# A fused attention, soft-MoE and top-1 MoE kernel: a new hand-written order, queries in four even quarters, an early exponential and shorter reader-less products

## The chip, the cores and the metric

The kernel runs on one core of a Trainium2 chip. The metric is the device time of one execution in microseconds (us). Engines are named as in the profile: PE (matrix products; PEld its weight loads), DVE (vector), ACT (scalar, exponentials), POOL (general), SP (here only the queue that issues most transfers).

## The reference, cut to what matters

```python
# q, k, v: (8 batches, 8 heads, 576 tokens, 64); x below: (4608 tokens, 512)
q_s = softmax(q, axis=-1)                    # over the 64 features
k_s = softmax(k, axis=2)                     # over the 576 tokens
kv  = einsum('bhsd,bhse->bhde', k_s, v)
x   = einsum('bhsd,bhde->bhse', q_s, kv)     # -> (4608, 512)

logits = x @ phi                             # (4608, 32): 8 experts x 4 slots
d = softmax(logits, axis=0)                  # over the tokens
slot_input = (d.T @ x).reshape(8, 4, 512)
for e in range(8):
    slot_out[e] = relu(slot_input[e] @ w1[e]) @ w2[e]
x = softmax(logits, axis=1) @ slot_out.reshape(32, 512)

g = x @ w_gate;  e_idx = argmax(g)           # a second MoE, top-1
gate = max softmax(g); eom = sigmoid(x @ w_output_gate)
out[token] = gate * eom[e_idx] * (relu(x @ m1[e_idx]) @ m2[e_idx])
```

Shapes: w1 is (8, 512, 1024), w2 is (8, 1024, 512), m1 and m2 are of the same shapes. All of it is float32.

## The kernel before

**Units.** The attention is done in 8 units of two batches by four heads; units 2p and 2p+1 (the two halves of the heads) make pair p, that is 1152 tokens. One load each of k, q and v for a unit is 1152 KB; after them come the 32 halves of expert weights (`lw.0` to `lw.31`, 1024 KB each, two of w1 and two of w2 for each expert), and late in the program the weights of the one expert that the second MoE picks (`lm`, `ln`). All these loads go through the queue of SP in the order in which the program writes them, and each load is written into a named buffer, its home. A home is used again and again: `W_HOMES` says into which buffer `lw.i` goes, and SP holds the load back until the last instruction that reads the old contents is done. Behind it every later load waits too. In the order before, `lw.9` goes to the buffer k0, which holds the v of unit 6 until then, last read by the product `kv.6.3`.

**Order.** Nothing is scheduled automatically. `ORDER` (attention and slots), `TAIL` (experts and the routing) and `LAST` are strings of short names; `do` walks through them and emits the instructions, and each engine runs its own in that order. After a colon stand the buffer of PSUM, the home or the engine of a copy (A is ACT, D is DVE):

```python
        for op in order.split():
            n, _, x = op.partition(":")
            n, *i = n.split(".")
            ops[n](*map(int, i), *(x.split(",") if x else ()))
```

The names that matter here, for unit u: `kmax`, `kexp` (DVE maximum, ACT exponential of k), `ktr`, `kev` (PE transposes and their copies to SBUF), `kv.u.x` (four groups of ten small products), `kve` (copy), `kvb`, `km`; for q `qmax`, `qsub` (POOL), `qexp`, `qsum`, `qrec`, `qmul` (POOL), `qtr`, `qev`; `lg` (logits of the pair into PSUM, bank L0). For a pair: `lmax`, `lexp`, `lcp` (a copy of the logits), `ll` (36 small products that turn the logits token by token), `le` (their copy to `l_all`), `ltr` and `lev` (transposes of the exponentials and their copy to `dz`), `su` (slot sums U), `m1` to `m6`, `uev`, `st`, `ute`, `sa`, `sc` (running maximum and sums over pairs). The last pair's `sc.3` closes `ORDER`; then come the experts: `i`, `in`, `j` (w1 products), `o` (w2 products), `G` (the routing that picks the expert whose weights `lm` and `ln` then load).

**Reader-less products.** `h` (function `hot`) writes products of a zero tile (`zero`) into a bank that nobody reads; `h.1.22` is 22 of 512 columns in bf16 and one of 264.

**Logits before.** A pair's 1152 tokens stand in four groups of PSUM partitions with 256, 320, 320 and 256 columns (`SEGS`), in a strip `LW` = 384 columns wide, of which the unused places hold -1e30 (a memset of `lp`).

**Output loop.** 36 tiles of 128 tokens, in 12 groups of three; each tile is four products of 512 columns; `drain` scales it (ACT and DVE in turn) and a store of 768 KB follows for each group. The last group's stores go out tile by tile.

**Constants.** The constants are built ahead of the manual schedule (`msched`), and the framework places them: three that are made from `ident` stand behind the first maxima of k on DVE.

## Time and profile before

| what | value |
|---|---|
| median of 3 runs | 220.82 us (220.55 to 221.08) |
| the profiled execution's own time | 220.66 us |
| its span in the trace | 218.9 us |
| PE busy | 207.6 us (95%) |
| DVE busy | 164.5 us (75%) |
| ACT busy | 115.8 us (53%) |
| POOL busy | 95.2 us (43%) |
| DMA | 76.30 MB, of it 66.42 MB read from HBM |
| granted TensorE clock, mean | 0.997 |

The span is what the hardware profiler saw from the first instruction to the last; the time of the execution is 1.76 us longer, and the prediction adds that to the span. Shares are means over a program with three stages: attention (to about 117 us), experts and routing (to about 177 us) and the output loop. PE's share holds the reader-less products too.

### The profile page before, as it was taken

The numbers are of one execution on the slowest core, as the hardware profiler recorded it, in microseconds if no ns is written. First come the engines' busy times: TensorE is split into PE (matmuls) and PEld (weight loads), VectorE is DVE, ScalarE is ACT, GpSimd is POOL, SyncE is SP. The second block draws the span as 40 slices with busy tenths as digits, with TensorE's granted clock in tenths as the row PEclk, the third lists the DMA queues.
The fourth block names the chain that finished last, engine by engine and source line by source line (L and its number), as shares of the span: only waits on it lengthen the run. The fifth ranks groups of instructions, "written<-read, shape, count | busy, mean of one in ns | idle before, by whom it ended". The sixth has DMA issues, their size and how long they took to land.

```text
span 218.9 us, 6486 instructions
## 1 busy us (share of the span) xinstructions
PE 207.6 (95%) x2649; PEld 151.5 (69%) x2649; DVE 164.5 (75%) x345; ACT 115.8 (53%) x262; POOL 95.2 (43%) x109
## 2 busy tenths in 40 slices
...
GB/s 225 425 423 421 418 419 414 419 419 417 417 423 412 412 415 424 394 106 418 428 415 418 413 416 419 418 412 422 403 410 164 0 52 252 249 268 237 287 276 165
DMA packets 12208, 76.30 MB, mean 349 GB/s; under 512 B 1488, under 2 KB 1872, under 8 KB 5392
## 3 DMA queue, kind: packets, MB, share of 16 engines
...
q10 hardware_dynamic: 288, 0.39, 0.5%
...
HBM read 66.42 MB, written 9.44 MB: 347 GB/s over the span
## 4 chain that ended last, share of the span: by engine, by line
PE 68%; DMA 22%; DVE 4%; ACT 2%; issue 1%; ACTq 1%; SPq 1%
DMA vz<-in_v_dram 9%; PE kv L284 7%; DMA we<-in_w_dram 7%; DMA vz<-in_w_dram 6%; PE p L393 5%; PE kv L1512 5%; PE L L1512 4%; PE p L261 4%; PE U L458 4%; PE U L644 3%; PE L L413 3%; PE U L795 2%; PE U L1512 2%; PE p L743 2%; PE kv L795 2%; PE kv L743 2%
## 5 line engine op out<-in xcount | busy, mean ns | idle before, releaser
L359 POOL TENSOR_TENSOR qt<-qt,qm 128x1280 f32<-128x1280 f32 (+1 forms) x14 | 29.5, 2118 | 14.0 <-DVE rk L310 8.0
L385 POOL TENSOR_TENSOR qt<-qt,qi 128x1280 f32<-128x1280 f32 (+1 forms) x14 | 29.5, 2117 | 2.9 <-DVE qi L374 1.9
L251 ACT ACTIVATE kt<-kt,km 128x576 f32<-128x576 f32 x28 | 21.6, 779 | 0.0
L244 DVE TENSOR_REDUCE km<-kt 128x4 f32<-128x2304 f32 (+1 forms) x10 | 18.1, 1823 | 3.1 <-DMA kt<-in_k_dram 3.1
L367 DVE TENSOR_REDUCE qeps<-qt 128x20 f32<-128x1280 f32 (+1 forms) x14 | 18.7, 1337 | 0.2 <-ACT qt L363 0.2
L772 POOL MEMSET hte<- 128x256 f32 x8 | 2.5, 315 | 37.7 <-DVE den L561 18.4
L352 DVE TENSOR_REDUCE qm<-qt 128x20 f32<-128x1280 f32 (+1 forms) x14 | 18.5, 1329 | 0.1
L363 ACT ACTIVATE qt<-qt 128x1280 f32<-128x1280 f32 (+1 forms) x14 | 16.2, 1178 | 2.7 <-POOL qt L359 2.6
L284 PE MATMUL kv<-ek,vt 128*64 128x64 f32 x384 | 15.5, 225 | 0.1
L284 PEld LDWEIGHTS kv<-ek,vt 128*64 128x64 f32 x384 | 13.2, 138 | 2.8 <-issue 2.4
L235 ACT COPY eT<-p 128x512 f32<-128x512 f32 (+1 forms) x22 | 11.6, 556 | 6.2 <-PE p L393 6.1
L261 PE MATMUL p<-ident,kt 128*128 128x128 f32 x98 | 14.1, 278 | 0.7 <-ACT kt L251 0.6
L393 PE MATMUL p<-ident,qt 128*128 128x128 f32 x96 | 13.6, 276 | 0.3 <-POOL qt L385 0.3
L644 PE MATMUL U<-zero 128*128 128x512 bf16 x42 | 11.7, 444 | 1.1 <-DVE zero L168 1.1
L261 PEld LDWEIGHTS p<-ident,kt 128*128 128x128 f32 x98 | 10.8, 140 | 2.6 <-ACT kt L251 1.3
L1512 PE MATMUL kv<-mst,hr 128*128 128x512 f32 (+1 forms) x30 | 11.6, 387 | 0.0
L1512 PE MATMUL L<-mst,hr 128*128 128x512 f32 (+1 forms) x30 | 11.5, 383 | 0.0
L393 PEld LDWEIGHTS p<-ident,qt 128*128 128x128 f32 x96 | 10.7, 142 | 1.0 <-POOL qt L385 0.5
L413 PE MATMUL L<-eT,mq 128*32 128x256 f32 (+1 forms) x128 | 10.8, 411 | 0.0
L458 PE MATMUL U<-qt,dz 128*32 128x256 f32 x140 | 10.7, 383 | 0.0
L644 PEld LDWEIGHTS <-zero 128*128 128x128 bf16 x49 | 5.4, 112 | 7.4 <-issue 3.0
L235 ACT COPY ek<-p 128x512 f32<-128x512 f32 x17 | 9.7, 585 | 0.9 <-PE p L261 0.9
...
## 6 DMA issues: line engine op xcount, KB each, us to landing
...
```

Source lines behind the costliest of these rows:

```text
L235: nc.scalar.copy(out=o, in_=i)
L251: nc.scalar.activation(out=t, in_=t, func=AF.Exp, bias=st_["km", u][:, x:x + 1], accum_out=st_["ksum", u][:, x:x + 1])
L261: nc.tensor.transpose(t[:, n * P:(n + 1) * P], ks_[u][:, j * P:(j + 1) * P], ident)
L284: nc.tensor.matmul(o[D * hh:D * hh + D, x * D:x * D + D], vt[:, f:f + D], kk, start=(n == 0), stop=(n == 4))
L352: nc.vector.tensor_reduce(out=m[:, :n], in_=t.rearrange("p (x d) -> p x d", d=D), op=ALU.max, axis=AX.X)
L359: nc.gpsimd.tensor_tensor(out=t, in0=t, in1=m.unsqueeze(2).to_broadcast([P, n, D]), op=ALU.subtract)
L367: nc.vector.tensor_reduce(out=qeps[u % 2 * 2 + x][:, :n, 0], in_=t.rearrange("p (x d) -> p x d", d=D), op=ALU.add, axis=AX.X)
L385: nc.gpsimd.tensor_tensor(out=t, in0=t, in1=s.unsqueeze(2).to_broadcast([P, n, D]), op=ALU.mult)
L393: nc.tensor.transpose(t[:, n * P:(n + 1) * P], qs_[u][:, o:o + P], ident)
L458: nc.tensor.matmul(U[NS * g:NS * g + NS, hf * HH * D:(hf + 1) * HH * D], dz[:, blk * P + NS * g:blk * P + NS * g + NS], t[:, j * HH * D:(j ...
L644: nc.tensor.matmul(scratch.rearrange("p (a b) -> p a b", a=2), zero[:, :P], zero[:, :2 * P].unsqueeze(1).to_broadcast([P, 2, 2 * P]), star ...
L1512: nc.tensor.matmul(op, a[:, x], w[:, d0:d1], start=False, stop=(k == 2))
```

## The change

The three strings and `W_HOMES` are written anew (most names stand elsewhere; most copies keep their engine). Beside that:

- The manual schedule starts ahead of the constants, so that they run in the order of the program, and one exponential of a constant, which nothing reads (`warm`), stands at the top of ACT.
- A pair's queries are laid out in four quarters of 288 tokens, so that the logits are four groups of 288 columns and `LW` is 288. With that `lcp`, `ll` and the old `le` give way to one DVE transpose of 32x32 blocks from PSUM into `l_all`; `ltr` has two PE transposes in place of three and the rest of `dz` is a DVE transpose of 128x32 (`ld`); `su` has twelve products a half in place of ten; `qev` writes the new layout. The memset of `lp` goes.
- The runs of reader-less products change; some of them are now float32 products of a constant tile (`bd`).
- The first four groups of the output are stored in two pieces, and of the last group's stores only the last goes through ACT's queue.

```diff
 ORDER = """
-kmax.0.1 kmax.0.0 kexp.0.1 kmax.0.2 kexp.0.0 h.1.22:U ktr.0.1:p0 kmax.0.3 kexp.0.2 ktr.0.0:p1 kev.0.1:D,eT0 kexp.0.3
+kmax.0.1 kexp.0.0 kmax.0.2 kexp.0.1 h.0.6.2:U ktr.0.0:p0 kmax.0.3 kexp.0.2 ktr.0.1:p1 kev.0.0:D,eT0 kexp.0.3 qmax.0.0
...
 W_HOMES = """
-eq0 z10 z01 z00 x0 eq1 eq2 q0 q1 k0 eT1 x1 eT0 eq4 k2 eq3 z11 k1 k3 eq0 z10 z11 x0 eq1 k0 eq2 eq4 eT0 eT1 k1 x1 k2
+k1 eq2 z00 z01 x0 k0 eq0 eq1 x1 eT0 q1 k3 eT1 eq4 k2 eq3 z11 q0 z10 k1 eq2 z11 x0 k0 eq0 eq1 x1 eT0 eq2 eq4 eT1 k3
 """.split()
...
+    msched = tc.manual_schedule()
+    msched.__enter__()
...
+    warm = const.tile([P, 1], F32, name="warm")
+    nc.scalar.activation(out=warm, in_=onec[:, 0:1], func=AF.Exp)
...
-    LW = 3 * P
-    SEGS = ((0, 256, 0), (256, 576, 0), (576, 896, 64), (896, 1152, 0))
+    LW = SP // 2
     lp = bank("L0")
-    nc.vector.memset(lp[:, :LW], -1e30)
...
-            for g, (n0, n1, o) in enumerate(SEGS):
+            for g in range(4):
                 nc.tensor.matmul(
-                    lp[NS * g:NS * g + NS, o:o + n1 - n0], mq[:, 2 * c + g // 2, :], e[:, c, n0:n1],
+                    lp[NS * g:NS * g + NS, :LW], mq[:, 2 * c + g // 2, :], e[:, c, g * LW:(g + 1) * LW],
...
-    def lcp(pr, eng):
-        t = at.tile([P, LW], F32, tag="ls", name="ls")
-        evac(eng, t, lp[:, :LW])
-        st_["ls", pr] = t
+    def le(pr):
+
+        nc.vector.transpose(
+            out=l_all[:, pr * RQ:(pr + 1) * RQ, :].rearrange("p r s -> p (r s)"), in_=lp[:, :LW]
+        )
...
-        for n in range(3):
+        for n in range(2):
             nc.tensor.transpose(t[:, n * P:(n + 1) * P], e[:, n * P:(n + 1) * P], ident)
...
+    def ld(pr):
...
+        nc.vector.transpose(out=st_["dz", pr][:, 2 * P:], in_=st_["ex", pr][:, 2 * P:])
...
-    def ll(pr, bk):
-
-        t, s = bank(bk), st_.pop(("ls", pr))
-        for r in range(RQ):
-            for b in range(2):
...
-    def hot(n, w, bk):
-
-        scratch = bank(bk)
+    def hot(n, w, *x):
+
+        scratch = bank(x[-1])
...
+        for _ in range(x[0] if len(x) > 1 else 0):
+            nc.tensor.matmul(scratch, bd[0][:, 0, :], bd[0].rearrange("p a b -> p (a b)"), start=True, stop=True)
...
-            store_all(g, t, t + 1, d0, d1, nc.scalar if eng == "A" else nc.sync)
+            store_all(g, t, t + 1, d0, d1, nc.scalar if eng == "A" and t == GT - 1 else nc.sync)
...
-            store_all(g, 0, GT)
+            cuts = (0, 1, GT) if g < HALVED else (0, GT)
+            for t0, t1 in zip(cuts, cuts[1:]):
+                store_all(g, t0, t1)
```

What the strings do to the engines is seen in their instructions. PE, near the end of the attention, before: the small products of units 6 and 7 (`kv0` and `kv1` are their banks; an 8 and a 2 of one unit are one `kv.u.x`), the last pair of rows for `kv0` being `kv.6.3`.

```order
L488 MATMUL p2_1557<-onec_82,mr_1546 32x1 x4
L437 MATMUL p0_1563<-ident_67,ex_1533 128x128 x3
L284 MATMUL kv1_1498<-ek_1340,vt_935 64x64 x8
L284 MATMUL kv1_1498<-ekz1_109,vt_935 64x64 x2
L284 MATMUL kv0_1205<-ek_1140,vt_349 64x64 x8
L284 MATMUL kv0_1205<-ekz0_103,vt_349 64x64 x2
L284 MATMUL kv1_1498<-ek_1340,vt_935 64x64 x8
L284 MATMUL kv1_1498<-ekz1_109,vt_935 64x64 x2
L284 MATMUL kv0_1205<-ek_1140,vt_349 64x64 x8
L284 MATMUL kv0_1205<-ekz0_103,vt_349 64x64 x2
```

After, the same place: `kv.6.3` is the third pair of rows, and what follows it are transposes of q of units 4 and 5 (L395, `qtr`), the last one of k of unit 7 (L263, `ktr.7.3`) and a slot step of pair 1 (L533).

```order
L286 MATMUL kv0_1117<-ek_1097,vt_781 64x64 x8
L286 MATMUL kv0_1117<-ekz0_107,vt_781 64x64 x2
L286 MATMUL kv1_1314<-ek_1278,vt_783 64x64 x8
L286 MATMUL kv1_1314<-ekz1_113,vt_783 64x64 x2
L286 MATMUL kv0_1117<-ek_1097,vt_781 64x64 x8
L286 MATMUL kv0_1117<-ekz0_107,vt_781 64x64 x2
L395 MATMUL p1_1367<-ident_71,qt_322 128x128 x4
L395 MATMUL p2_1381<-ident_71,vz1_298 128x128 x4
L395 MATMUL L1_1387<-ident_71,qt_322 128x128 x2
L395 MATMUL p0_1390<-ident_71,vz1_298 128x128 x4
L263 MATMUL p1_1396<-ident_71,kt_722 128x128 x4
L533 MATMUL p2_1406<-s2_1364,U_sb_1264 128x64 x4
```

So `kv.6.0` to `kv.6.3` moved ahead of nine `qtr`, of `lg.4` and `lg.5` and of `ktr.7.3`. The homes changed with that: the k0 of `lw.9` was freed by `kv.6.3`; now `lw.8` takes the buffer of unit 6's v (x1, freed by `kv.6.3`), `lw.9` that of unit 6's exponentials (eT0, `kv.6.3` too), `lw.10` that of unit 7's k (q1, freed by `ktr.7.3`), `lw.11` and `lw.12` those of unit 7 that `kv.7.3` frees.

DVE at the start, before: memsets, the four maxima of the first k (`km`), then three constants made from `ident`, then the first copies of transposed k (`ek`).

```order
L163 MEMSET sum2_76 128x64
L168 MEMSET zero_80 128x132
L170 MEMSET onec_82 128x128
L202 MEMSET L0_112 128x384
L244 TENSOR_REDUCE km_142<-kt_117 128x1 x4
L159 TENSOR_REDUCE idr_72<-ident_67 128x32
L161 COPY sum4_74<-idr_72 128x128
L165 COPY sum2_76<-idr_72 64x32 x2
L237 COPY ek_185<-p0_173 128x512
```

After: the constants stand ahead of the first maximum, and the memset of the logits' bank (L202) is gone.

```order
L160 MEMSET zero_69 128x132
L164 MEMSET onec_76 128x128
L169 MEMSET sum2_80 128x64
L171 TENSOR_REDUCE idr_82<-ident_71 128x32
L173 COPY sum4_84<-idr_82 128x128
L175 COPY sum2_80<-idr_82 64x32 x2
L246 TENSOR_REDUCE km_141<-kt_118 128x1 x4
L239 COPY ek_169<-p0_157 128x512
```

DVE behind the last logits, before: copy of the logits (`ls`), maximum (`lm`), a copy of the slot sums (`U_sb`), copy to `l_all`, the step L479 and half of `dz`.

```order
L237 COPY ls_1768<-L0_112 128x384
L420 TENSOR_REDUCE lm_1770<-L0_112 128x1
L237 COPY U_sb_1795<-U_1733 128x512
L237 COPY l_all_86<-p0_1775 128x288
L479 TENSOR_REDUCE mr_1809<-p2_1797 1x32
L237 COPY dz_1811<-L1_1799 128x192
```

After: the maximum comes first, then the two DVE transposes that take the place of the copies; the copies of `dz` are on ACT.

```order
L328 TENSOR_TENSOR mq_1645<-L1_1621,rk_1112 128x128
L422 TENSOR_REDUCE lm_1671<-L0_116 128x1
L433 STREAM_TRANSPOSE l_all_90<-L0_116 128x288
L455 STREAM_TRANSPOSE dz_1685<-ex_1674 128x32
L487 TENSOR_REDUCE mr_1689<-p2_1677 1x32
```

## Rows read from the trace of the kernel before

**Rows 1.** the page's first line.
```profile
span 218.9 us, 6486 instructions
```

**Rows 2.** busy time by stretch: microseconds, each engine, TensorE clock, DMA share, GB/s.
```profile
3.00:92.30 89.30, 87.85 (x1333) 70.11 (x1331) 85.29 (x130) 79.56 (x177) 67.86 (x45) 1.00 1.01 418
92.30:98.30 6.00, 6.00 (x133) 5.58 (x132) 3.47 (x10) 1.99 (x7) 5.80 (x7) 1.00 0.41 116
98.30:165.50 67.20, 65.55 (x936) 40.28 (x938) 40.70 (x107) 12.84 (x39) 12.46 (x34) 1.00 1.01 416
```

**Rows 3.** waits of the load queue SP: total, times, longest.
```profile
SPq L602 <- PE kv L284: 17.8, 3, 9.7
```

**Rows 4.** timeline of SP's queue around the pause: start, duration, instruction.
```profile
86.17 0.33 SPq L602 DMA_DIRECT2D we<-in_w_dram  x1
...
96.27 0.33 SPq L602 DMA_DIRECT2D we<-in_w_dram  x1
```

**Rows 5.** groups by line and form, whole span: busy, mean ns | idle before.
```profile
L458 PE MATMUL U<-qt,dz 128*32 128x256 f32 x140 | 10.7, 383 | 0.0
L575 PE MATMUL p<-ident,ls 128*64 128x32 f32 x108 | 3.7, 223 | 0.0
...
L237 DVE COPY eT<-p 128x512 f32<-128x512 f32 x9 | 6.2, 688 | 0.7 <-PE p L393 0.5
L237 DVE COPY ls<-L 128x384 f32<-128x384 f32 x3 | 1.7, 558 | 3.2 <-PE L L413 3.2
L237 DVE COPY ekz<-p 64x256 f32<-64x256 f32 x2 | 0.9, 428 | 0.1
L1033 DVE STREAM_TRANSPOSE kx<-p 128x512 f32<-128x512 f32 x1 | 0.7, 716 | 0.0
L237 DVE COPY l_all<-p 128x288 f32<-128x288 f32 x1 | 0.5, 459 | 0.5 <-PE p L575 0.5
L1033 DVE STREAM_TRANSPOSE kx<-p 128x128 f32<-128x128 f32 x1 | 0.3, 318 | 0.0
```

**Rows 6.** timeline at the start, first exponential and constants.
```profile
4.78 1.28 ACT L251 ACT_TABLE_LOAD   x1 [4.78 <-DMA kt<-in_k_dram]
7.47 0.36 DVE L159 TENSOR_REDUCE idr<-ident 128x32 f32<-128x128 f32 x1
...
8.01 0.36 DVE L165 COPY sum<-idr 64x32 f32<-64x32 f32 x2
```

**Rows 7.** busy time from the first data on.
```profile
12.83:92.00 79.17, 77.72 (x1281) 64.58 (x1280) 77.52 (x116) 72.90 (x162) 65.87 (x42) 1.00 1.01 418
```

**Rows 8.** busy time where short transposes start.
```profile
8.40:10.20 1.80, 1.80 (x19) 1.80 (x18) 1.28 (x2) 1.44 (x5) 0.00 (x0) 1.00 1.05 430
8.30:22.00 13.70, 12.96 (x132) 9.18 (x132) 12.88 (x17) 10.69 (x24) 7.70 (x4) 1.00 1.02 424
```

**Rows 9.** the same stretch, lines L644 and L649 alone (reader-less products).
```profile
8.30:22.00 13.70, 4.51 (x21) 1.96 (x20) 1.00 1.02 424
...
8.30:22.00 13.70, 2.38 (x18) 1.66 (x17) 1.00 1.02 424
```

**Rows 10.** timelines: first routed-weight load, last w2 product, the gather.
```profile
150.49 0.35 SPq L973 DMA_DIRECT2D vz<-in_m_dram  x1
...
156.32 2.19 PE L795 MATMUL U<-we,hte 128*32 128x512 f32 x16
...
172.47 0.46 POOL L1143 TENSOR_TENSOR ra<-oh,kx 128x128 f32<-128x128 f32 x1 [1.21 <-DVE rmx L1153]
173.42 1.26 POOL L1396 DMA_INDIRECT kx<-in_m2r_dram,idx  x1 [0.50 <-DVE z L1146]
```

**Rows 11.** busy time in the output loop.
```profile
177.40:212.80 35.40, 35.39 (x161) 29.17 (x161) 23.89 (x56) 16.78 (x30) 1.78 (x4) 1.00 0.59 237
```

**Rows 12.** timeline of ACT's next to last store and last tile.
```profile
211.77 1.28 ACTq L1478 DMA_DIRECT2D out_dram<-ob  x1
...
213.09 0.47 ACT L761 ACTIVATE ob<-kv,gates 128x256 f32<-128x256 f32 x1 [1.35 <-PEq L1536]
```

More of the change, by code (lines that the diff above doesn't have):

```diff
@@ new lines @@
+ktr.0.2:p2 kev.0.1:A ktr.0.4:L1 ktr.0.3:p0 kev.0.2:A kev.0.5:D kev.0.4:A qsub.0.0 kev.0.3:D krk.0 krr.0 kmax.1
+qexp.0.0 qmax.0.1 kexp.1.0 kexp.1.2 qsum.0.0 h.0.3.4:U ktr.1.0:p1 qsub.0.1 kexp.1.1 ktr.1.2:p2 qmax.1.0 kev.1.0:A,eT1
+ktr.1.1:L1 kev.1.2:A kev.1.1:A qadd.0.0 qmax.1.1 qexp.0.1 qsub.1.0 h.0.2:U kv.0.0 kexp.1.3 qrec.0.0 qsum.0.1 kv.0.1
+krk.1 ktr.1.4:p0 ktr.1.3:p1 krr.1 qmul.0.0 qexp.1.0 qadd.0.1 kev.1.4:D kv.0.2 lv.2:x0 lk.4:eq2 lv.3:z10 lq.5:z11
+lk.5:z00 lv.4:z01 lk.6:k0 qrec.0.1 kmax.3 kv.0.3 kev.1.3:A kev.1.5:A lq.4:k2 kve.0:A qmul.0.1 h.0.1:U qtr.0.0:p2
@@ new lines @@
+qtr.0.1:L1 qsum.1.0 qev.0.0:A,eq3 kv.1.0 qev.0.1:A kbd.0 kexp.3.1 qtr.0.2:p1 qadd.1.0 qtr.0.3:p0 kexp.3.0 qsub.1.1
+qev.0.2:D kvb.0:p2 qtr.0.4:L1 qev.0.3:D kexp.3.2 ktr.3.0:p1 kvbe.0:D qev.0.4:A kv.1.1 kev.3.0:A,eT0 qrec.1.0 kmax.2
+qexp.1.1 ktr.3.2:p0 qmul.1.0 ktr.3.1:L1 kev.3.2:A kv.1.2 kev.3.1:A km.0:p2 kexp.3.3 qsum.1.1 kv.1.3 kexp.2.2
+qtr.1.1:p1 kmq.0 kexp.2.1 qadd.1.1 ktr.2.2:p0 kve.1:D qrec.1.1 qtr.1.0:L1 kexp.2.3 qmax.2.1 kbd.1 ktr.2.1:p2 krk.3
+kev.2.2:A,eT1 lg.0 qmul.1.1 kev.2.1:D kexp.2.0 qmax.2.0 km.1:p0 krk.2 qev.1.1:A,eq3 kvb.1:p2 qsub.2.1 qev.1.0:A kmq.1
@@ new lines @@
+qtr.1.2:p1 krr.2 qmax.3.0 kvbe.1:A ktr.2.0:p0 qev.1.2:A ktr.2.3:L1 kev.2.0:A ktr.2.4:p2 qtr.1.4:p1 qsub.2.0 kev.2.3:D
+qexp.2.1 qtr.1.3:p0 qev.1.4:D ktr.3.3:L1 kev.2.5:D qev.1.3:A ktr.3.4:p1 kmax.4 kev.3.3:A lg.1 kev.3.4:A qsub.3.0
+kev.2.4:A qexp.2.0 kv.2.0 kev.3.5:A lmax.0 kv.2.1 kexp.4.0 qmax.3.1 kv.3.0 kexp.4.3 kv.2.2 krr.3 qsum.2.0 qsub.3.1
+kexp.4.1 kv.3.1 m1.0:p0 kexp.4.2 ktr.4.0:L1 m2.0 ktr.4.3:p2 qadd.2.0 lexp.0 qmax.5.0 ktr.4.2:p1 krk.4 qexp.3.0
+ltr.0:p0 kv.3.2 ld.0 qrec.2.0 qsub.5.0 kv.2.3 le.0 lev.0:A qexp.3.1 qsum.3.0 kv.3.3 lv.5:x0 lq.6:q0 lk.7:q1 ktr.4.1:p0
@@ new lines @@
+st.0:L1 krk.5 kev.5.4:A kev.5.5:A qmul.2.1 qtr.3.1:p0 qev.3.0:A,eq4 ute.0 qtr.3.2:p2 krr.5 qev.3.1:A qmax.4.1
+qtr.3.3:p1 qev.3.2:A ktr.5.1:L1 qev.3.3:A qtr.3.4:p0 qsub.4.0 krr.4 qsum.5.1 qtr.2.2:p2 kev.5.1:A qtr.2.3:p1 qev.3.4:A
+qev.2.2:A qtr.2.4:L1 kmax.6 ktr.5.3:p0 qev.2.4:A kv.5.0 qev.2.3:A lw.2 qsub.4.1 kev.5.3:A kv.4.3 qexp.4.0 kv.5.1 lw.3
+qadd.5.1 lg.2 kve.4:D kexp.6.0 qsum.4.0 kbd.4 sa.0:p2 kexp.6.3 lg.3 kexp.6.1 sc.0 qrec.5.1 qadd.4.0 qmax.6.1 kexp.6.2
+qmul.5.1 ktr.6.0:L1 ktr.6.3:p1 qexp.4.1 ktr.6.4:p0 le.1 kvb.4:p2 qrec.4.0 kev.6.4:D,eT0 kev.6.0:A kv.5.2 qmul.4.0
```

171 lines of the change are left out of this document (71 added, 100 removed).

## The prediction

> **What bounds the kernel now.** I read the busy time by stretch first, then the queue of loads, then single rows. The profiled execution took 220.66 us, 0.16 below the median of 220.82; its span is 218.9 [rows 1], so 1.76 us lie around it, and the sum is made against 220.66. From 3 us to 92.3 the loads run at 418 GB/s with a DMA share of 1.01, and from 98.3 to 165.5 at 416 [rows 2]. The loads are a stream without air, and the reader is to see the one hole in it: between 92.3 and 98.3 only 116 GB/s moved [rows 2]. The queue of SP shows why. It issued one load of weights at 86.17 and the next, `lw.9`, at 96.27 [rows 4], and of the nearly ten microseconds between them 9.7 were a wait for PE's `kv` products [rows 3]: `lw.9` must not overwrite the v of unit 6 before `kv.6.3` has read it. The full rate came back at 98.3, 2.0 us behind the issue. The hole cost 6.00 x (1 - 116/418) = 4.3 us of loading.
>
> Behind the hole the stream is full again to 165.5, the end of the routed expert's weights, and the last w2 product stands inside it, at 156.32 [rows 10]. The experts' end therefore hangs on the stream; routing and output loop follow it. In the output loop PE is busy for 35.39 of 35.40 us at a DMA share of 0.59 [rows 11], so that stage is PE's and the stores have room.
>
> Ahead of the hole the engines are nearly as full as the stream: from 12.83 to 92 DVE is busy for 77.52 of 79.17 us and PE for 77.72 [rows 7]. A load can therefore be late because the work that frees its buffer is late.
>
> **The change, part by part.**
>
> *The hole.* In the new order of PE, `kv.6.3` stands ahead of nine `qtr`, `ktr.7.3`, `lg.4`, `lg.5`, and the three `ll` that stood ahead of it are gone. By the stretch in which 19 products (18 of them transposes) filled 1.80 us [rows 8], a transpose is worth 0.1 us. Nine `qtr` are some 34 transposes, 3.4 us; `ktr.7.3` 0.4; three `ll` 108 x 3.7/108 = 3.7 [rows 5]; the two `lg`, 32 records, 2.4 at the 10.7/140 = 0.076 us of a similar 32-row record [rows 5]. That is 9.9 us, and 96.27 - 9.9 = 86.4; since DVE's work does not shrink as much, I take 87 with 1.5 to either side. `lw.8` and `lw.9` now hang on it. To leave no hole, `lw.9` has to be issued 2.0 us before 92.3, at 90.3, and a megabyte lasts 1.05/0.418 = 2.5 us, so `lw.10` is due at 92.8, `lw.11` at 95.3. `ktr.7.3` follows `kv.6.3` within a few transposes, `kv.7.3` only shortly before the last logits. The latter I place at 95 to 96, so some tenths of a hole may be left there. Of the 4.3 us I take **4.0**; bounds 0 (the hole only moves) and 4.3.
>
> *The logits' new shape.* DVE loses three copies of 0.558, one of 0.459 and three of `dz` (two whole, one half) which I price like the former, -1.40; together -3.5 [rows 5]. It gains four transposes of 288 columns, between the 0.318 of 128 columns and the 0.716 of 512 [rows 5], by width about 0.48 each, and four of 32 columns, between nothing and 0.318, say 0.2: +2.7. Moved evictions: four fewer of 512 columns at 0.688, six more small ones at 0.428 [rows 5], -0.2. Sum -1.0 us. The constants that filled DVE from 7.47 to 8.37, 0.9 us, now run while DVE waits for the first k, and the 1.28 us table load leaves the first exponential [rows 6]. DVE's work to the end of the attention is thus about **1.9 us** shorter; with the transposes at their bounds (1.3 to 4.1) it is 0.5 to 3.3. PE loses 144 records of `ll`, 4.9 us, and four transposes, 0.4; it gains 16 products of `su`, 32 records, between nothing (if their column groups overlap) and 2.4. All this lies under the stream of loads and is worth nothing by itself; it is what lets the attention keep up with a stream that no longer stops. Without it the gain of the hole is cut, as the first rival says.
>
> *Behind the experts.* The weights of the routed expert are issued from 150.49 [rows 10], still a queue's length ahead of the stream's need. If the w loads end 4.0 us sooner, around 153.4 by the last w2 product, they need to be issued 2 us ahead of that: an issue at the old 150.49 still does. In the routing POOL's L1143 at 172.47 takes 0.46 just ahead of the gather at 173.42 [rows 10]; the new order has it elsewhere. Bounds nothing and 0.5, since the gather also waits for DVE; I take **0.2**.
>
> *The output.* Splitting four stores costs queue time in a stage with DMA to spare [rows 11]: nothing; if that cover went, the 0.3 us of an issue [rows 4] each. At the end, ACT's queue is held by the issue of a store from 211.77 for 1.28 us, and the last tile of ACT starts behind it at 213.09 [rows 12]. The store now goes through SP. ACT can start as soon as its product is done, but DVE's half of the tile and its store end at about the same time: between nothing and 0.6, I take **0.2**.
>
> *The reader-less products.* From 8.3 to 22 PE is busy for 12.96 us at a granted clock of 1.00 [rows 8], of them 4.51 + 2.38 = 6.9 in products that nobody reads [rows 9]. Fewer columns are streamed now. Where the clock stays, the cost is nothing: the engine is not what ends that stretch. In the 1.80 us after the first run, PE did almost nothing but transposes and the clock stayed at 1.00 [rows 8], the higher of its levels of 1.2 and 2.4 GHz. The Trainium skill, "TensorE: Matmul & The Clock Gate", section "Part 4: PE-mode transpose", says that transposes do not count as busy for the clock in the same way and that the full clock does not engage for them; that speaks against shortening these runs. By the row, nothing is added; by the rule, the clock rival below.
>
> Sum: 220.66 - 4.0 - 0.2 - 0.2 = 216.26, given as **216.3 us**.
>
> **The rivals.**
>
> *The attention takes the place of the hole.* The hole closes, but the work of the engines, which filled 98% of the time to 92 us, comes forward only by DVE's 1.9 us. Behind it PE is busy for 65.55 of 67.20 us [rows 2], so little can be caught up. For it speaks that `kv.7.3`, the last logits and the running sums follow each other through several engines; against it that part of PE's time there is reader-less and waits for weights. Time: 220.66 - 1.9 - 0.2 = 218.5.
>
> *The hole only moves.* Another home (`lw.10` or `lw.11`) waits as long as k0 did. For it: five loads in a row still hang on the last two units. Against it: 9.9 us of PE's work went behind `kv.6.3`. Time: 220.5, no change.
>
> *More comes back.* PE's 4.9 us of `ll` shorten the end of the attention too, and the experts run ahead into the stream's end: 1.5 to 2 us below the forecast, about 214.5.
>
> *Slower, by the clock.* The clock falls to the lower level behind the first, shorter run, and stays there to 22 us. The 6.1 us of real work (12.96 - 6.9) would take 6.1 more, and the reader-less products twice theirs, some 2 us above what they took. The attention would end 8 us later than it would, against the 4.0 + 1.9 gained: 220.66 + 8 - 5.9 = 222.8. It decides from the point where more than about 5 us are lost. Against it: the clock row above.
>
> *Slower, by the routing.* The products of the next experts stand elsewhere, and `G` is late: every microsecond by which the routed weights are issued after 151.4 (153.4 less the 2.0 of a restart) costs one, and 155.8 is the point from which the kernel is slower; at 156.4, six us behind the old issue, it ends at 221.3.
>
> **How the numbers follow.** Forecast 216.3 (own range 215.2 to 217.6): 0.57. Attention in the hole's place, 218.5 (217.6 to 219.6): 0.20. More comes back (under 215.2): 0.07. The hole only moves, 220.5: 0.05. Clock, 222.8: 0.06. Routing, 221.3: 0.05. From 214.6 to 219.6 stand the first two and most of the third, 0.8. A measurement of this kernel can tell about 0.2%, 0.44 us, from no change. Faster by more: 0.57 + 0.20 + 0.07 = 0.84; within it: 0.05; slower: 0.11.
>
> **What would show it.** Right: the stretch from 92 to 98 us carries over 400 GB/s, SP's waits for `kv` have no entry of nine microseconds, `lw.9` is issued by 90.3, the last w2 product starts near 152.3, the output loop near 173.2 and lasts as long. Wrong: full loads, but a last w2 product later than 155 (the attention or the experts' products bind); a hole at another place in SP's waits; a granted clock under 0.9 between 8 and 22 us; routed weights issued after 151.4.

## The result, and the profile after

The changed kernel took 217.56 us (median of 4 executions, 217.33 to 217.98) against 220.95 us (4, 220.55 to 221.09) for the kernel before: a ratio of 0.9851, interval 0.9833 to 0.9868. The forecast was 216.3 us; 3.4 us were gained where the sum had 4.4. In ten further executions (below) the changed kernel took 217.2 to 219.3 us in six and 220.8 to 228.3 us in four, at a lower mean TensorE clock, and every ratio here leaves out executions like those four. With all ten counted the median is 219.0 us against 220.9 for the kernel before beside them, a gain of 1.9 us and not of 3.4.

The profiled execution of the changed kernel took 217.33 us. The first line of its page, against [rows 1]:

```profile
span 215.4 us, 6199 instructions
```

Its busy time by stretch, with the columns of [rows 2] (PE, PEld, DVE, ACT, POOL, then clock, DMA share and GB/s):

```profile
3.00:92.30 89.30, 85.32 (x1302) 65.54 (x1301) 84.79 (x134) 76.37 (x169) 69.79 (x46) 1.00 1.01 425
92.30:98.30 6.00, 6.00 (x82) 4.99 (x80) 4.41 (x11) 4.28 (x12) 4.02 (x6) 1.00 1.01 425
12.83:92.00 79.17, 75.85 (x1266) 60.41 (x1265) 76.45 (x124) 70.76 (x156) 66.39 (x42) 1.00 1.01 425
174.40:209.00 34.60, 34.60 (x160) 28.76 (x158) 23.12 (x55) 16.83 (x30) 1.85 (x4) 1.00 0.59 243
```
The hole of [rows 2] is gone: 92.3 to 98.3 us moved 425 GB/s where it was 116. The stretch ahead of it runs at 425 too, where it was 418, which the prediction had not foreseen. From 12.83 to 92 us PE and DVE are still nearly full, as in [rows 7], and the output loop is PE's, as in [rows 11]. By the rates, the closed hole is worth 6.00 x (1 - 116/425) = 4.4 us of loading and the higher rate ahead of it 89.3 x (1 - 418/425) = 1.5.

SP's waits for `kv` products, which answer to [rows 3]: those of the weight loads (L590) have no entry of nine microseconds left. One load of v (L233), issued at 46.13 us, does wait 11.0, where that of before waited 8.4; the loads run at 424 GB/s from 40 to 50 us all the same, so it makes no hole. Here a long wait of the queue was a hole only where the loads already issued ran out.

```profile
SPq L590 <- PE kv L286: 6.1, 2, 5.1
SPq L233 <- PE kv L286: 11.0, 1, 11.0
```
The timeline at the places of [rows 4] and [rows 10]: two loads of weights, the last `acc` step of the attention, the first routed-weight load, the last w2 products, the gather, and a product of the loop's first tile:

```profile
83.44 1.05 SPq L590 DMA_DIRECT2D we<-in_w_dram  x1
...
93.65 0.33 SPq L590 DMA_DIRECT2D we<-in_w_dram  x1
...
112.28 0.35 DVE L568 SCALAR_TENSOR_TENSOR acc<-acc,w,L 128x128 f32<-128x128 f32 x1 [1.04 <-PE L L560]
...
148.07 0.35 SPq L960 DMA_DIRECT2D vz<-in_m_dram  x1
...
151.96 0.64 PE L782 MATMUL p<-we,hte 128*32 128x512 f32 x4
...
169.31 1.26 POOL L1383 DMA_INDIRECT kx<-in_m2r_dram,idx  x1 [1.83 <-DVE z L1140]
...
173.79 0.50 PE L1474 MATMUL kv<-mst,cstack 128*128 128x512 f32 x1 [0.38 <-DVE lr L1449]
```
What the reader is to see: `lw.9` is issued at 83.44 us (before: 96.27) and `lw.11` at 93.65, with loads enough in the queue that nothing stops. The last w2 products start at 151.96 (before: 156.32), the gather at 169.31 (173.42). But the loop's product at 173.79 waits for the `lr` steps of DVE, not for the gather.

The attention's end in the timeline of before:

```profile
116.27 0.35 DVE L560 SCALAR_TENSOR_TENSOR acc<-acc,w,p 128x128 f32<-128x128 f32 x1 [1.04 <-PE p L552]
```
The difference by stages, from the same marks in both timelines (start of the row unless it says end, us; PE's last product starts at 212.54 and 208.72 and takes 0.28):

| mark | before | after | difference |
|---|---|---|---|
| last `acc` step, the attention's end | 116.27 | 112.28 | -3.99 |
| `so_b`, behind the last w2 product | 158.56 | 154.02 | -4.54 |
| first product of the output loop (L1512, now L1500) | 177.99 | 174.36 | -3.63 |
| end of PE's last product | 212.82 | 209.00 | -3.82 |
| end of the span | 218.9 | 215.4 | -3.5 |

So the part up to the experts gave 4.5 us, the routing gave back 0.9, the loop won 0.2, and the end gave back 0.3. The stream itself came forward by more: the last expert weights landed at 151.20 where it was 157.42, 6.2 us sooner, and the last w2 products no longer wait for them.

### The profile page after: what moved, and what is told of

It is laid out like the page before. It is cut to its first block, busy times and chain, and to the rows that moved or that the text cites. A ratio compares the mean times of both kernels' runs of the same rounds, so it can differ in the third digit from the quotient of the medians.

```text
span 215.4 us, 6199 instructions
## 1 busy us (share of the span) xinstructions
PE 201.3 (93%) x2500; PEld 141.9 (66%) x2500; DVE 160.5 (75%) x347; ACT 115.4 (54%) x260; POOL 95.6 (44%) x109
## 4 chain that ended last, share of the span: by engine, by line
PE 62%; DMA 19%; DVE 10%; ACT 2%; SPq 2%; issue 1%; DVEq 0%
DMA vt<-in_v_dram 8%; PE kv L286 6%; PE p L395 5%; PE kv L1500 5%; PE L L1500 5%; DMA vz<-in_w_dram 5%; PE kv L782 4%; PE U L467 4%; DMA w2q<-in_m_dram 4%; PE p L730 3%; PE L L415 3%; PE p L263 2%; DMA kt<-in_k_dram 2%; PE U L1500 2%; DVE km L246 2%; DVE qm L354 2%
## 5 line engine op out<-in xcount | busy, mean ns | idle before, releaser
L361 POOL TENSOR_TENSOR qt<-qt,qm 128x1280 f32<-128x1280 f32 (+1 forms) x12 | 25.3, 2118 | 10.3 <-DVE qm L354 9.1
L387 POOL TENSOR_TENSOR qt<-qt,qi 128x1280 f32<-128x1280 f32 (+1 forms) x12 | 25.3, 2118 | 1.3 <-DVE qi L381 1.1
L354 DVE TENSOR_REDUCE qm<-qt 128x20 f32<-128x1280 f32 (+1 forms) x12 | 16.0, 1331 | 0.0
L369 DVE TENSOR_REDUCE qeps<-qt 128x20 f32<-128x1280 f32 (+1 forms) x12 | 15.9, 1328 | 0.0
L263 PE MATMUL p<-ident,kt 128*128 128x128 f32 x92 | 14.2, 279 | 1.4 <-ACT kt L253 1.0
L365 ACT ACTIVATE qt<-qt 128x1280 f32<-128x1280 f32 (+1 forms) x12 | 14.2, 1180 | 2.1 <-POOL qt L361 2.1
L263 PEld LDWEIGHTS p<-ident,kt 128*128 128x128 f32 x92 | 10.2, 140 | 4.7 <-ACT kt L253 4.0
L395 PE MATMUL p<-ident,qt 128*128 128x128 f32 x86 | 12.5, 278 | 0.6 <-POOL qt L387 0.6
L1500 PE MATMUL kv<-mst,hr 128*128 128x512 f32 (+1 forms) x30 | 11.5, 385 | 0.0
L1500 PE MATMUL L<-mst,hr 128*128 128x512 f32 (+1 forms) x30 | 11.5, 384 | 0.0
L395 PEld LDWEIGHTS p<-ident,qt 128*128 128x128 f32 x86 | 9.5, 141 | 2.1 <-POOL qt L387 0.9
L691 ACT CAST st<-l_all 128x256 fp32r<-128x256 f32 x9 | 3.6, 407 | 12.4 <-PE U L708 6.5
L361 POOL TENSOR_TENSOR vz<-vz,qm 128x1280 f32<-128x1280 f32 (+1 forms) x4 | 8.5, 2118 | 3.8 <-issue 1.9
L467 PE MATMUL U<-qt,dz 128*32 128x256 f32 (+1 forms) x144 | 9.8, 385 | 0.0
L1449 DVE SCALAR_TENSOR_TENSOR lr<-p,hr 128x384 fp32r<-128x384 f32 x11 | 6.1, 556 | 4.8 <-ACT hr L1446 4.8
L415 PE MATMUL L<-eT,mq 128*32 128x288 f32 x128 | 9.4, 412 | 0.0
```

What stands on the lines that cost most here:

```text
L263: nc.tensor.transpose(t[:, n * P:(n + 1) * P], ks_[u][:, j * P:(j + 1) * P], ident)
L354: nc.vector.tensor_reduce(out=m[:, :n], in_=t.rearrange("p (x d) -> p x d", d=D), op=ALU.max, axis=AX.X)
L361: nc.gpsimd.tensor_tensor(out=t, in0=t, in1=m.unsqueeze(2).to_broadcast([P, n, D]), op=ALU.subtract)
L369: nc.vector.tensor_reduce(out=qeps[u % 2 * 2 + x][:, :n, 0], in_=t.rearrange("p (x d) -> p x d", d=D), op=ALU.add, axis=AX.X)
L387: nc.gpsimd.tensor_tensor(out=t, in0=t, in1=s.unsqueeze(2).to_broadcast([P, n, D]), op=ALU.mult)
L395: nc.tensor.transpose(t[:, n * P:(n + 1) * P], qs_[u][:, o:o + P], ident)
```

## Experiments

Each starts from the changed kernel; what it changes stands in its first lines (`...` stands for lines or names left out).

**The hole put back.** `lw.8` to `lw.10` are written behind `kv.7.3`, and two homes are exchanged:

```diff
-qtr.4.3:p1 lw.8 lw.9 qadd.6.1
+qtr.4.3:p1 qadd.6.1
...
-m3.2:p0 lw.11 lw.12
+m3.2:p0 lw.8 lw.9 lw.10 lw.11 lw.12
...
-k1 eq2 z00 z01 x0 k0 eq0 eq1 x1 eT0 q1 k3 eT1 eq4 ...
+k1 eq2 z00 z01 x0 k0 eq0 eq1 k3 eT0 q1 x1 eT1 eq4 ...
```

> The changed kernel with the hole put back: lw.8, lw.9 and lw.10 are written behind kv.7.3, and lw.8 takes the buffer that kv.7.3 frees (lw.11 takes that of lw.8). Nothing else moves. In the changed kernel lw.8 was issued at 83.0 us; here it can be only at about 93.6. Theory (the stream of loads sets the end of the experts): lw.8 lands 4.7 us behind its issue, at 98.3 in place of 94.5, every later load is 3.8 us late, and of that 0.8 us is slack that the last w load now has ahead of the last w2 product; 217.6 + 3.0 = 220.6 us. Rival (what brought the gain is the shorter work of the engines, and the stream is no longer what binds): 217.6 to 218.4 us, with a hole in the loads to be seen all the same.

Measured: 224.14 us (223.27 to 224.94), ratio to the kernel before 1.0146 (1.0118 to 1.0173); more than either theory said. Its stretches, with the columns as above, and its timeline:

```profile
80.00:92.30 12.30, 12.30 (x232) 10.60 (x229) 11.38 (x25) 6.59 (x14) 12.30 (x6) 1.00 0.79 332
92.30:98.30 6.00, 6.00 (x81) 4.93 (x79) 4.35 (x11) 4.22 (x12) 4.00 (x6) 1.00 0.59 216
120.60:124.00 3.40, 3.40 (x22) 1.31 (x21) 0.00 (x0) 0.80 (x3) 0.00 (x0) 0.50 1.00 424
```
```profile
93.59 0.33 SPq L590 DMA_DIRECT2D we<-in_w_dram  x1
...
112.22 0.35 DVE L568 SCALAR_TENSOR_TENSOR acc<-acc,w,L 128x128 f32<-128x128 f32 x1 [1.04 <-PE L L560]
...
119.63 0.43 PE L730 MATMUL p<-vz,sT 128*32 128x128 f32 x8 [4.01 <-DMA vz<-in_w_dram]
...
140.14 0.33 SPq L590 DMA_DIRECT2D we<-in_w_dram  x1
```
The attention ends at 112.22, as in the changed kernel: the engines' work is untouched. The loads stop, since `lw.8` is issued at 93.59: 332 GB/s from 80 to 92.3 and 216 from 92.3 to 98.3, where the changed kernel has 424 and 425, are 12.3 x (1 - 332/424) + 6.0 x (1 - 216/425) = 5.6 us of loading. So this hole is longer than the 4.3 us of the kernel before: three loads wait here for `kv.7.3`. Then PE stands still for 4.01 us for a load at 119.6, the clock falls to its lower level for 3.4 us, and another load is held back to 140.14, because the experts that must free its buffer are late. `so_b` starts at 160.09, 6.1 us late, about what the hole took; what the later stop and the clock cost beside it isn't told apart. The stream binds: with the attention's end untouched, a hole in the loads costs the experts' end all of its length. That this kernel is slower than the one before goes with its longer hole.

**Work added on PE.** `h.11.0` ahead of each `ltr`:

```diff
-ltr.0:p0
+h.11.0:p0 ltr.0:p0
```

> The changed kernel with eleven reader-less products of 264 columns (some 1.2 us) on PE ahead of each of the four ltr, the place of the old ll: 4.8 us of PE work are back in the attention. Theory (PE's own chain sets the end of the attention, and the experts follow it): the attention ends 3.5 to 4.8 us later and the time is 220.6 to 222.4 us. Rival (DVE sets the pace, or only the stream of loads): at most 1.2 us, that of the last pair, 217.6 to 218.8 us.

Measured: 222.76 us (222.55 to 225.06), ratio 1.0108 (1.0070 to 1.0145). The last `acc` step of its timeline, and the stretch of the hole:

```profile
118.37 0.35 DVE L568 SCALAR_TENSOR_TENSOR acc<-acc,w,L 128x128 f32<-128x128 f32 x1 [1.04 <-PE L L560]
```
```profile
92.30:98.30 6.00, 6.00 (x96) 4.68 (x89) 4.50 (x18) 2.49 (x9) 5.88 (x6) 1.00 0.87 341
```
The four runs, priced at 4.8 us (the trace has each busy for 1.40, 5.6 together), moved the attention's end by 6.1 us, and the loads slow down again (341 GB/s), since `kv` products that free buffers come later. Work at the place of the old `ll` is on the path.

**Work added on DVE.** Three copies of the logits behind each `lmax`, read by nothing:

```diff
+    def lcp(pr):
+        t = at.tile([P, LW], F32, tag="ls", name="ls", bufs=1)
+        for _ in range(3):
+            nc.vector.tensor_copy(out=t, in_=lp[:, :LW])
```

> The changed kernel with three copies of the logits on DVE behind each lmax, which nothing reads: 12 x 0.46 = 5.5 us of DVE work are added at the place of the old lcp. If DVE sets the pace of the attention (the prediction's price of 1.9 us for its end rests on that): 3.5 to 5.5 us more, 221 to 223 us. If PE does: only the last pair's 1.4 us, which stand directly in the chain of its slot sums, 218.5 to 219.3 us.

Measured: ratio 1.0078 (1.0036 to 1.0120); the profiled execution took 221.72 us, the other three 221.91, 224.26 and 232.88. Its last `acc` step:

```profile
116.70 0.35 DVE L573 SCALAR_TENSOR_TENSOR acc<-acc,w,L 128x128 f32<-128x128 f32 x1 [1.04 <-PE L L565]
```
5.5 us of work on DVE moved it by 4.4. The two runs together say that the attention has no single engine that sets its pace: work added at these places on either counts for most of its length or more. My expectation, which set one against the other, was too simple.

**The old places of three routing steps.** `q.3` (with `q.1`) goes behind the first `b`, `l.0` (with `l.2`) behind the last `a`, and `lc.0` with its gates behind `b.2`:

```diff
-... q.3 h.1.0:L0 a.0:kv0 q.1 a.1:p1 ac.0:D
-l.0:p2 ac.1:D b.0:L1 lc.0 h.1.0:L0 b.1 ga.0.0 a.2:p0 ga.0.2 ...
+... h.1.0:L0 a.0:kv0 a.1:p1 ac.0:D
+ac.1:D b.0:L1 q.3 h.1.0:L0 b.1 q.1 a.2:p0 ...
```

> The changed kernel with three steps of the routing put back to where they stood before: q.3 behind the first b, l.0 behind the last a, lc.0 with its gates behind b.2. Theory (the 0.9 us that the routing gave back are these products, which stand ahead of a.0 and of b.0 on PE): the first product of the output loop starts 0.6 to 0.9 us earlier, 216.7 to 217.0 us. Rival (the loop's start hangs on the gather or on the lr steps, which take the time up): within 0.2 us of 217.6.

Measured: ratio 0.9885 (0.9845 to 0.9926), no better than the changed kernel's 0.9851. The first `b`, the first `k` and the loop's first product in its timeline:

```profile
158.42 0.33 PE L1297 MATMUL L<-rcols,s_sb 128*128 128x73 f32 x1
...
164.34 0.64 PE L1415 MATMUL L<-w2q,kx 128*32 128x512 f32 x4 [0.26 <-POOL kx L1340]
...
175.44 0.39 PE L1500 MATMUL kv<-mst,hr 128*128 128x512 f32 x1
```
The first `b` starts 1.04 us earlier than in the changed kernel (159.46), but the first `k` 0.43 later (163.91) and the loop 1.08 later (174.36). The moved steps do stand in the way of `b`, but with them at the old places the later steps start later. The theory falls; the order after is the better one of these two, although the routing as a whole takes longer than before.

**The start of before.** No early exponential, and the constants behind the first maxima:

```diff
-    warm = const.tile([P, 1], F32, name="warm")
-    nc.scalar.activation(out=warm, in_=onec[:, 0:1], func=AF.Exp)
...
-kmax.0.3 kexp.0.2
+kmax.0.3 cst kexp.0.2
```

> The changed kernel with the start of before: the three constants made from ident stand behind the first maxima of k on DVE, and the early exponential is gone, so that the table load (1.28 us) lies ahead of the first real exponential again. Theory (the chain of DVE and PE up to the attention's end decides, as the two kernels with added work showed with 0.8 to 1.2 us for each us added): the attention ends 0.6 to 1.5 us later, 218.2 to 219.1 us. Rival (the prediction's: worth nothing by itself, since it lies under the loads): within 0.3 us of 217.6.

Measured: 219.16 us in the profiled execution (217.33 in the changed kernel's), two more at 219.67 and 219.77 and four between 222.12 and 229.48; ratio 0.9965 (0.9915 to 1.0015). The stretch of the first loads, and two marks:

```profile
3.00:92.30 89.30, 85.03 (x1300) 65.27 (x1299) 85.69 (x138) 77.24 (x170) 69.63 (x46) 1.00 1.01 418
```
```profile
112.44 0.35 DVE L562 SCALAR_TENSOR_TENSOR acc<-acc,w,L 128x128 f32<-128x128 f32 x1 [1.04 <-PE L L554]
...
155.89 0.43 DVE L974 TENSOR_TENSOR so_b<-p,so_g 128x256 f32<-128x256 f32 x1 [2.06 <-PE p L782]
```
A surprise: the attention ends only 0.16 us later, but the loads run at 418 GB/s, as in [rows 2], and not at 425, and `so_b` starts 1.9 us later, behind PE's wait for a w2 product that itself waits for its load. Both reasons that I had were wrong. 418 in place of 425 is 1.5 us of loading by 92.3, and the last expert weights land at 154.68, 3.5 us later; the start matters by the loads' rate. Which of the two edits does it, and how, no run shows.

**No early reader-less products.** `h.0.6.2`, `h.0.3.4`, `h.0.2` and `h.0.1` are taken out of the attention.

> The changed kernel without the four runs of reader-less products in the attention. Theory (they hold the clock): the granted clock is at its lower level in part of the first 25 us, PE falls behind by up to half of what it does there, 219 to 222 us. Rival (the clock comes up by the real work alone): the clock is as before from 10 us on and the time within 0.5 us of 217.6, or below it by up to 1 us, since some PE work is gone.

Measured: 221.01 us in the profiled execution, six executions between 218.68 and 222.74, ratio 0.9913 (0.9875 to 0.9952). Two stretches, the transposes of k up to 18 us (least, median and greatest ns), and two marks:

```profile
3.00:18.00 15.00, 7.38 (x38) 6.35 (x40) 12.86 (x15) 10.06 (x23) 5.43 (x6) 1.00 1.02 424
168.50:178.60 10.10, 10.02 (x29) 5.59 (x29) 3.61 (x9) 2.23 (x5) 1.50 (x2) 0.50 0.09 26
```
```profile
L263 PE MATMUL p<-ident,kt x24: 421/421/476, 6.2 to 16.1; 128*128 128x128 f32 x24
```
```profile
112.02 0.35 DVE L568 SCALAR_TENSOR_TENSOR acc<-acc,w,L 128x128 f32<-128x128 f32 x1 [1.03 <-PE L L560]
...
177.52 0.63 PE L1500 MATMUL kv<-mst,hr 128*128 128x512 f32 x1
```
The same transposes in the changed kernel:

```profile
L263 PE MATMUL p<-ident,kt x24: 272/273/331, 6.4 to 15.3; 128*128 128x128 f32 x24
```
421 ns against 273: PE runs at the lower level through its first 17 us, although the column of the clock reads 1.00 there. It costs nothing: the attention ends 0.3 us earlier than in the changed kernel, for PE is busy for only 7.38 of these 15 us. The time is lost elsewhere: from 168.5 to 178.6 us the clock stands at 0.50, and the loop starts at 177.52, 3.2 us late. All six executions have a mean clock of 0.971 or less, which is some 13 us or more at the lower level in each (an estimate: 219 x 0.029 x 2, since the lower level is half of the full one), so the other five lost it too. The early products are not needed where they stand, but without them the clock was lost every time; how the two hang together no run shows.

**No reader-less products in the experts' stage.** The ten runs between `xt` and `o.7.1` are taken out.

> The changed kernel without the ten small runs of reader-less products between the attention's end and the last w2 product (together some 1.7 us of PE). Theory (PE's chain sets the experts' stage now, the stream being 0.8 us ahead of it): the last w2 product comes forward by up to the 0.8 us that the stream leaves, 216.8 to 217.3 us. Rival (they lie in waits of PE): within 0.2 us of 217.6. Second rival (the clock falls without them): slower, with a granted clock below 0.95 in slices 20 to 29.

Measured: 217.55 us in the profiled execution, ratio 0.9825 (0.9779 to 0.9871). Its `so_b`:

```profile
154.08 0.42 DVE L974 TENSOR_TENSOR so_b<-p,so_g 128x256 f32<-128x256 f32 x1 [2.25 <-PE p L782]
```
154.08 against 154.02: they lie in waits of PE, as the rival said. Three of its four executions took 217.23 to 217.91 us, one 221.03.

**The old rule for the last stores.**

```diff
-            store_all(g, t, t + 1, d0, d1, nc.scalar if eng == "A" and t == GT - 1 else nc.sync)
+            store_all(g, t, t + 1, d0, d1, nc.scalar if eng == "A" else nc.sync)
```

> The changed kernel with the old rule for the stores of the last group: all of ACT's tiles store through ACT's queue. The prediction gave the new rule 0.2 us (0 to 0.6). If that is right: 217.6 + 0.2 = 217.8 us, with ACT's last tile held back by the issue of a store, as in the trace of before. Rival (the new rule costs, since three stores on SP drain one behind the other: from PE's end to the end of the span it is 6.4 us in the changed kernel and 6.1 before): 217.2 to 217.4 us.

Measured: 217.28 us in the profiled execution, three executions between 216.44 and 217.28, three between 221.54 and 222.86, ratio 0.9789 (0.9743 to 0.9835). That speaks rather for the rival, but the first three lie 0.8 us apart. In the trace ACT's last tile is held back by the issue of a store, as the expectation said (it starts at 209.28, the changed kernel's at 208.57), and the end comes 6.7 us behind PE's last product, where it is 6.4. The section on the output below says why neither the gain nor the cost of the rule can be read from this pair.

This profiled execution has something else: the clock fell in the attention.

```profile
16.50:19.90 3.40, 3.10 (x39) 2.14 (x39) 3.40 (x5) 2.95 (x7) 2.52 (x2) 0.50 1.02 431
```
The attention ends at 112.11 even so (112.28 in the changed kernel).

**The changed kernel again.**

> The changed kernel itself, unchanged, more often. In the runs so far its relatives spread far more than the kernel before: the one with the old end rule differs in nothing that PE does, and three of its six executions took 221.5 to 222.9 us at a mean clock of 0.963 to 0.967, the others 216.4 to 217.3 us at 0.982 to 0.996, while 27 executions of the kernel before stayed between 220.3 and 222.5 us at 0.991 or more. Theory (the changed kernel, with its shorter reader-less runs, is prone to a fall of the TensorE clock, as the clock rival said, but only in some executions): two to four of ten executions above 220 us at a mean clock under 0.975, the rest at 217.3 to 218.0. Rival (the spread comes from what the experiments changed): all of them at 217.3 to 218.0 us and 0.99 or more.

Measured: six of ten executions between 217.22 and 219.29 us at a mean clock of 0.982 to 0.997, four between 220.80 and 228.28 at 0.931 to 0.972; 15 of the kernel before, taken beside them, lie between 220.58 and 221.66 at 0.992 to 0.998. So the changed kernel itself has these executions, four of fourteen with the first four counted, and the kernel before had none in 53, all at 0.991 or more. The ratio of the other six is 0.9870 (0.9846 to 0.9894). None of the four was profiled. By their mean clock they stood at the lower level for some 12 to 31 us in all (an estimate: 219 x 0.028 x 2 and 226.5 x 0.069 x 2; the level is half of the full one); in which stage isn't shown.

**Reader-less products added**, to see where the clock falls: two in the routing, ten between 16 and 24 us, and both (the first two edits together).

```diff
-ga.0.6 h.0.1:L0 4.1
+ga.0.6 h.0.2:L0 4.1
...
-k.1.3 ga.0.8 rw.1
+k.1.3 ga.0.8 h.0.1:L0 rw.1
```

```diff
-h.0.2:U kv.0.0
+h.0.5:U kv.0.0
...
-h.0.1:U qtr.0.0:p2
+h.0.4:U qtr.0.0:p2
...
-kv.1.0
+h.0.4:U kv.1.0
```

> The changed kernel with two more reader-less products of 512 columns in the routing, at places where PE waits for POOL and for DVE (166.6 and 167.9 us in its trace). In the profiled execution without the early runs the clock fell at 168.4 and stayed at the lower level for 10.2 us, which made the output loop start 3.2 us later. Theory (the fall in the routing is what makes the slow executions): none or one execution above 220 us, and the fast ones at 217.3 to 218.2 us. Rival (the falls lie in the first 25 us): as many above 220 us as the changed kernel itself in the same call.

> As the kernel with two more reader-less products in the routing, and ten more of 512 columns at three places between 16 and 24 us, where PE waits for the first v and for POOL. If falls at both places make slow executions: no execution above 220 us here, some in the kernel with the routing's products alone. If only the routing's falls do: like that kernel. If neither: as many as the changed kernel itself. The fast executions: 217.3 to 218.2 us.

> The changed kernel with the ten early reader-less products alone (three places between 16 and 24 us), and none in the routing. The kernel with both took 216.2 to 216.9 us in all of five executions at a clock of 0.996 or more; the one with the routing's two alone still fell (its profiled execution at 157.7 us, for 6.8 us, ahead of both added products). Theory (the early stretch is where slow executions come from): no execution above 220 us, the fast ones near 216.2 us. Rival (the falls are the routing's, and both sets of products or chance kept them away): one to three of some six executions above 219 us at a clock below 0.985. Of the end: if the 1.2 us by which the kernel with both ended sooner behind its last product come from where PE's program is fetched, this kernel, with eleven products more than the changed one, ends like it, 5.5 us behind its last product, and not 6.4 to 6.7.

(The early products are ten, not eleven.) Measured: with the routing's two, 216.84 to 219.48 us in five executions and 229.85 in one, ratio 0.9851 (0.9826 to 0.9877); with the early ten, 216.18 to 219.26 in five and 220.89 in one, ratio 0.9855 (0.9815 to 0.9896); with both, 216.16 to 216.86 in all five, median 216.19, ratio 0.9796 (0.9783 to 0.9809), at a clock of 0.996 or more. The profiled executions of the first two had a fall, in the same stretch of the routing; the stretches with the routing's products alone, with the early ones alone, and with both, and the loop's first product in the first two:

```profile
157.70:164.50 6.80, 6.80 (x49) 2.91 (x37) 2.81 (x10) 1.12 (x5) 0.63 (x2) 0.50 0.47 189
```
```profile
158.00:165.00 7.00, 7.00 (x51) 3.02 (x43) 3.00 (x10) 1.30 (x5) 0.82 (x2) 0.52 0.47 192
```
```profile
157.70:164.50 6.80, 6.52 (x83) 3.44 (x73) 4.95 (x19) 1.99 (x8) 1.91 (x4) 1.00 0.45 185
```
```profile
176.73 0.39 PE L1500 MATMUL kv<-mst,hr 128*128 128x512 f32 x1
...
177.09 0.40 PE L1500 MATMUL kv<-mst,hr 128*128 128x512 f32 x1
```
Three of the profiled falls lie in the routing (the third in the run without early products, at 168.5), and the loop starts 2.4 to 3.2 us later with them; one lay at 16.5 (the old rule for the last stores) and one behind the stop of the run with the hole. The early products alone don't prevent a fall, and the two in the routing, at 166.6 and 167.9, come after the fall at 157.7. Why none fell with both, in five executions, is open: the changed kernel had none in its first four executions either, so chance may do it. The kernel with both is the fastest here, but not by its products: in the profiled executions PE's last product ends at 208.89 us with both and at 209.00 in the changed kernel, and the rest of the 1.1 us between them comes at the end of the span (below).

## Why the prediction was right, and where its sizes were off

**How near the edge.** The range ended at 217.6 us, where the first rival's began, and the median was 217.56; of fourteen executions in all four lie below 217.6. That the range was kept is in part luck. The loads' rate, which rose with the start and which the prediction put at nothing, brought 1.9 us at `so_b`, while the routing and the end gave back 1.2 that it had not foreseen. With the old start the same order took 219.2 to 219.8 us in its three quickest executions: the first rival's time, though not by the rival's reason, for the attention ended within 0.2 us of the changed kernel's. Of the signs set down for being right, the loads, the issue of `lw.9` and the last w2 products came (425 GB/s, 83.4, 151.96 where 152.3 was said); the loop's start did not (174.36 where 173.2 was said).

**The hole** (forecast -4.0 up to the experts' end; measured -4.54 at `so_b`). Right, by its own step: `kv.6.3` came ahead, `lw.9` went out at 83.4 where 87 was forecast and 90.3 needed, and putting a hole back, a longer one, costs the whole gain and 3 us more. `kv.6.3` came 13 us sooner, not 9.9: the sum of what moved behind it left out `kv.7.2` and `ltr.2`, and what the fewer reader-less products save; the rest isn't taken apart. The stage gained more than forecast because the loads run at 425 GB/s in place of 418, 1.5 us by 92.3, and that goes with the start. Hole and rate together are 5.8 us of loading, of which 4.54 came out: the last expert weights land 0.8 us ahead of the last w2 products (151.20 and 151.96), so at its end the stage no longer hangs on the stream, where the prediction had it hang.

**"Worth nothing by itself, it lets the attention keep up."** For the logits' new shape that holds, and the two runs with added work show how hard the condition is: of some 5 us put back on either engine, 4.4 to 6.1 came out at the attention's end. The first rival priced the attention's end by DVE's 1.9 us alone, 218.5; PE's 4.9 us of `ll` counted as well, and the end came 4.0 us sooner. For the start, "worth nothing" failed: undoing it costs 1.8 us, by the loads' rate and not by the engines.

The prices of the new operations held. The two DVE transposes, in the groups by form (busy, mean ns), against 0.48 and 0.2 us forecast:

```profile
L433 DVE STREAM_TRANSPOSE l_all<-L 128x288 f32<-128x288 f32 x4 | 1.8, 460 | 0.3 <-ACT ex L428 0.3
L455 DVE STREAM_TRANSPOSE dz<-ex 128x32 f32<-128x32 f32 x4 | 0.8, 194 | 0.7 <-PE p L482 0.7
```
**Behind the experts** (forecast -0.2; measured +0.9). The step about the gather was right and beside the point: it follows its index by 0.45 us where it was 0.81, but the loop's first product waits for `lr` instead. What failed is the unspoken rest of the step, that the routing keeps its length. The timeline of the routing, first before, then after:

```profile
158.56 0.42 DVE L987 TENSOR_TENSOR so_b<-U,so_g 128x256 f32<-128x256 f32 x1 [1.66 <-PE U L795]
...
161.31 0.44 PE L1299 MATMUL L<-vz,soT 128*32 128x256 f32 x4
...
162.68 0.33 PE L1310 MATMUL p<-rcols,s_sb 128*128 128x73 f32 x1
...
177.99 0.39 PE L1512 MATMUL kv<-mst,hr 128*128 128x512 f32 x1
```
```profile
154.02 0.42 DVE L974 TENSOR_TENSOR so_b<-p,so_g 128x256 f32<-128x256 f32 x1 [1.00 <-PE p L782]
...
156.79 0.40 PE L1000 MATMUL kv<-wgo,soT 128*128 128x16 f32 x2
...
157.46 0.42 PE L1286 MATMUL kv<-vz,soT 128*32 128x256 f32 x4
...
158.46 0.63 PE L1012 MATMUL p<-cstack,gst 64*32 64x512 f32 x4
...
159.46 0.33 PE L1297 MATMUL L<-rcols,s_sb 128*128 128x73 f32 x1
...
174.36 0.40 PE L1500 MATMUL kv<-mst,hr 128*128 128x512 f32 x1
```
From `so_b` to the first `a` it was 2.75 us and is 3.44, with `q.3` at 156.79 and a reader-less product ahead of it; from there to the first `b` 1.37 and now 2.00, with `l.0` at 158.46 ahead; some of it is won back later, and the loop starts 20.34 us behind `so_b` where it was 19.43. That these products delay `b` is shown by the run with the old places (the first `a` starts 0.23 us earlier there, the first `b` 1.04); that undoing them would pay is refuted by it.

**The output** (forecast -0.2; measured +0.3 from PE's end to the span's: 6.4 us where it was 6.1). The transfers by queue in the last 9.5 us tell more than the rule of the stores: in the changed kernel, then in the kernel with both sets of added products, where queue q8 has no row there (count, MB and share of the queue; KB and median us to landing of the store):

```profile
q8 instruction: 1, 0.02, 0.8%
out_dram<-ob ACTq DMA_DIRECT2D x1, 128.0 KB, 4.7
```
```profile
out_dram<-ob ACTq DMA_DIRECT2D x1, 128.0 KB, 3.2
```
In the first a 16 KB fetch of program code (queue q8) stands among the last stores, and ACT's 128 KB store takes 4.7 us to land; in the second the store takes 3.2 us, and the span ends 5.5 us behind PE's last product and not 6.4. The other traces agree: where the q8 fetch falls between 1.8 us ahead of the end of PE's last product and 2.9 us behind it (ten profiled executions) the span ends 6.0 to 6.7 us behind that product; with the new rule and no such fetch (both sets, the early ten alone, work added on PE) it ends 5.5 to 5.8 behind. The kernel before has no such fetch and ends 6.1 behind. So the new rule may well be worth its 0.2 us or a little more, and what the end gave back goes with where the fetch falls. The runs with it under the old and the new rule end alike (6.7, and 6.0 to 6.7). That the fetch is the cause is argued from these traces, and no run isolates it.

**The clock rival** had the price wrong. Early, the lower level costs nothing (no early products: attention at 112.02; old rule for the last stores: at 112.11). In the routing, a stage for which the prediction has no such term, a fall came in three profiled executions of the kernel's relatives, at 2.4 to 3.2 us apiece. The rival's chance of 0.06 was for a fall in every execution; four of fourteen executions of the changed kernel were as slow as the kernel before or slower, at a lower mean clock, and no trace shows where they lost it. Which edit made the kernel prone to it is open: the old places of `q.3` and `l.0` don't cure it (two of six executions there took 222 and 224 us).

The Trainium skill, "TensorE: Matmul & The Clock Gate", section "Part 4: PE-mode transpose", says that transposes don't bring up the full clock. The run without early products agrees: up to 17 us PE had only transposes, at 421 ns each, with PE half idle, so that the two reasons aren't told apart. Once the clock was up, 1.80 us of transposes did not lower it [rows 8]. What the rule would make of the time (222.8 by the rival) did not come, for PE has time to spare there.
